# A planner's row of background work: a mark ends a slot only behind work, and four marks for a chunk instead of eight

## The chip, the core and the metric

The kernel runs on one core of a Trainium2 chip. What counts is the device time of one execution in microseconds (us). The core has a matrix engine (TensorE, in the rows PE for the matmuls and PEld for the loading of their stationary operand), a vector engine (VectorE, DVE), a scalar engine (ScalarE, ACT), a general one (GpSimd, POOL) and a queue that starts the DMAs (SyncE, SP). Each engine works off its own queue in program order, and semaphores make it wait for the others.

## The reference, cut to what matters

Three stages follow one another: an attention with 32 memory slots for each head, a feed-forward stage, and a stage of four experts, in which every token goes through every expert. Only the last is touched here:

```python
def _moe2_ref(x, domain_probs, w1, w2):      # x 2304 x 512, w1 4 x 512 x 1024, w2 4 x 1024 x 512
    p = domain_probs / (domain_probs.sum(-1, keepdims=True) + 1e-09)
    out = np.zeros((N, D), dtype=np.float32)
    for e in range(E):
        h = np.maximum(x @ w1[e], 0.0)
        out += p[:, e:e + 1] * (h @ w2[e])
    return out
```

## The kernel before, in words

All matmuls work on numbers that are split in two: a high part `hi` that TensorE takes in its fast format, which ScalarE writes with a cast, and the rest `lo`, which VectorE writes by subtracting `hi` from the number. A product of two split numbers is three matmuls (`PASSES`): hi by hi, hi by lo, lo by hi. So every weight needs a `hi` on ScalarE and then a `lo` on VectorE before its matmuls can run.

The expert stage goes through the tokens in three passes of 768 tokens (two halves of 384). A pass has eight chunks, so there are 24 chunks, n = 0 to 23: half of one expert's 1024 hidden columns each. A chunk consists of:

- two **units**, m = 2n and 2n+1 (`unit`). Each multiplies a 2 x 2 block of `w1` with the 2 x 2 block of x in the manner of Strassen, seven products instead of eight, each of six matmuls of 384 columns. The products come in the order b, a, c, d, a, c, d, named by the PSUM bank that they go to (`pb`, `pa`, `pc`, `pd`); the second ones of a, c and d add to what stands in their bank. Between them ScalarE copies bank b to `p` (L915), VectorE forms `u` twice (a plus p, then c plus that; L906) and the sums `cy`, `cx`, and the two engines make the eight `h` tiles of the chunk (L879, L880). The second product of a may start only when VectorE has read a for the first `u`.
- the **second** half (`second`): h by `w2`, six blocks of twelve matmuls of 512 columns, in PSUM tiles `po` (L954). After each block VectorE adds the scaled result to `oacc` (L962).

The weights are prepared beside this as background work. For a unit m these are the four casts `hi0`, `hi3`, `hi2`, `hi1` (L320), the four subtractions `lo0`, `lo3`, `lo2`, `lo1` (L323), and on GpSimd the four additions `s1`, `s3`, `s2`, `s4` (L326 to L335), which form from the raw blocks the sums that Strassen's scheme wants. `hi2` and `lo2` need s1 and s3, `hi1` and `lo1` need all four, and s1 may overwrite its block only when lo0 and lo3 have read theirs. For `w2` there are four casts (L351) and four subtractions (L355) a chunk. In the rows the tiles are `W_0` to `W_3` (or `pair`, where the half-size W_3 lies in a shared tile) and `w_n_q`. Four DMAs a chunk bring the raw weights into a ring of four buffers.

All these pieces stand in one list, `todo`, in an order written out by hand. `fill(t)` takes pieces from its head in a **slot**, until t us of VectorE time are used up or a mark (`gap`) comes. There are slots only at certain places of a chunk: one after the first product of a unit, b, and one after its second product, a (t = 0.6; the other five products have t = 0, with which `fill` does nothing), and one after each of the six blocks of the second half (t = 1.9). That makes ten slots a chunk. What is not yet done when it is needed is done at once by `need(key)`, which takes everything ahead of it from the list as well. A piece that needs a free weight slot and finds none also ends `fill`. A piece done in a slot lands on its engine's queue behind everything that stands there already.

Behind the last chunk of a pass, the x tiles of the next pass (`x_ops`, 18 pieces, L683, L686, L689) are put ahead of the list.

Of the kernel before, what the change touches and what calls it, by code (L numbers as in the profile page):

```python
# [126 lines left out]
def body(ctx: ExitStack, tc: tile.TileContext, phiT, kv, qT, w_in, w_out, w1, w2, dp, out):  # L127
# [635 lines left out]
    def add(key, t, ok, fn):  # L763
        todo.append((key, t, ok, fn))

    def go():
        key, t, ok, fn = todo.pop(0)
        assert ok(), key
        fn()
        made.add(key)  # L770
        return t

    def fill(t):
        while todo and t > 0 and todo[0][2]():
            if todo[0][0] == "gap":
                todo.pop(0)
                break
            t -= go()

    def need(key):  # L780
        while key not in made:
# [14 lines left out]
    def gap():  # L796
        todo.append(("gap", 0, yes, None))
# [3 lines left out]
    def add_unit(m, *names):  # L801
        if m not in steps_of:
            steps_of[m] = unit_ops(m)
        for name, eng, cost, fn in steps_of[m]:
            if name in names:
                ok = has_half if name == "hi3" else has_slot if eng == "A" else yes
                add((name, m), cost / 1e3 if eng == "V" else 0, ok, fn)

    def add_w2(step, n, x):
        for q in (2 * x, 2 * x + 1):  # L810
            add((f"w2{step}", n, q), 0.6 if step == "lo" else 0, has_slot if step == "hi" else yes,
                partial(w2_lo if step == "lo" else w2_hi, n, q))

    def load(fn, *a):

        if a[0] <= (last_n if fn is w2_load else 2 * last_n + 1):
            add(("load", fn.__name__, *a), 0, yes, partial(fn, *a))
# [9 lines left out]
    add_w2("hi", 0, 0)  # L827
    gap()
    add_unit(1, *B2)
    gap()  # L830
    add_w2("lo", 0, 0)
    load(w2_load, 1, 0)
    load(unit_load, 3)
    add_w2("hi", 0, 1)
    add_unit(2, *A1)
    gap()
    add_w2("lo", 0, 1)
    load(w2_load, 1, 1)
    gap()
    for n in range(1, last_n + 1):  # L840
        m = 2 * n
        add_unit(m, *A2)
        add_w2("hi", n, 0)
        gap()
        add_w2("lo", n, 0)
        gap()
        add_unit(m, *B1)
        add_unit(m + 1, *A1)
        gap()
        add_unit(m, *B2)  # L850
        load(unit_load, m + 2)
        load(w2_load, n + 1, 0)
        gap()
        add_unit(m + 1, *A2)
        add_w2("hi", n, 1)
        gap()
        add_w2("lo", n, 1)
        gap()
        add_unit(m + 1, *B1)
        if n < last_n:  # L860
            add_unit(m + 2, *A1)
        gap()
        add_unit(m + 1, *B2)
        load(unit_load, m + 3)
        load(w2_load, n + 1, 1)
        gap()

    late_lo = []

# [13 lines left out]
    def unit(n, u):  # L883
# [25 lines left out]
        def step(t):  # L909
            flush(1)  # L910
            fill(t)
# [29 lines left out]
    def second(n, half):  # L941
        p, c = divmod(n, NCE)
        e = c // (FF2 // CF)
        t = 2 * p + half
        if c == 0:
            oacc[t] = acc_slot(t, [P, TW // P, DM], f"oacc{t}")
        for q in range(4):
            need(("w2lo", n, q))
        for j in range(TW // P):
            ps = ps_acc.tile([P, DM], F32, tag=f"acc{blk[0] % 4}", name="po")  # L950
            blk[0] += 1
            for i in (0, 2, 3, 1):
                for k, (x, y) in enumerate(PASSES):
                    nc.tensor.matmul(ps, hts[n, i, half][0][:, x, j * P:(j + 1) * P], w2s[n, i][0][:, y],  # L954
                                     start=(i == 0 and k == 0), stop=(i == 1 and k == 2))
            flush(0)
            o, tt = oacc[t][:, j], t * (TW // P) + j
            sc = pr[:, tt, e:e + 1]
            if c == 0:
                nc.vector.tensor_scalar_mul(o, ps, sc)  # L960
            else:
                nc.vector.scalar_tensor_tensor(out=o, in0=ps, scalar=sc, in1=o, op0=ALU.mult, op1=ALU.add)  # L962
            if c == NCE - 1:
                nc.sync.dma_start(out=out[tt * P:(tt + 1) * P, :], in_=o)
            fill(1.9)
        for i in range(4):
            h_free.append(hts.pop((n, i, half))[1])
        if half == 0:
            for i in range(4):
                free_slots.append(w2s.pop((n, i))[1])  # L970
# [46 lines left out]
```

## Time and profile before

| what | value |
|---|---|
| three runs | 1214.91 us median, 1214.39 to 1219.59 |
| profiled execution, its own time | 1214.46 us |
| its span in the trace | 1212.7 us, of which the expert stage fills 391.8 to the end |
| TensorE | busy 1135.1 us, 94% of the span |
| VectorE, ScalarE, GpSimd | busy 849.9, 466.1 and 173.5 us |

The profiled execution is 0.45 us under the median, and its span is 1.8 us shorter than its own time, since a little lies before and behind the trace. TensorE's busy time counts overlapped matmuls, so what can be read from a stretch is the distance from one start to the next.

### The profile page before, as it was taken

How to read it: one execution, taken by the hardware profiler on the slowest of the kernel's cores; microseconds unless marked ns; L12 is line 12 of the kernel's file. 1: busy time of each engine (PE TensorE's matmuls, PEld its weight loads, DVE VectorE, ACT ScalarE, POOL GpSimd, SP SyncE). 2: the span in 40 equal slices, each digit the busy share in tenths (PEclk: the TensorE clock that was granted, in tenths of full speed). 3: DMA queues.
4: the chain of work that ended last, by engine and by line, in shares of the span. 5: the costliest groups of instructions: out<-in, count | busy, mean ns of one | idle time of the engine just before them, and what ended most of it. 6: DMA issues, size and time to landing. Idle time of an engine off the chain costs nothing. (4 is left out here: it accounts for less than half of the span.)

```text
span 1212.7 us, 16585 instructions
## 1 busy us (share of the span) xinstructions
PE 1135.1 (94%) x6488; PEld 1031.6 (85%) x6488; DVE 849.9 (70%) x1510; ACT 466.1 (38%) x918; POOL 173.5 (14%) x200
## 2 busy tenths in 40 slices
PE   4999999999999999999998799999998799999998
PEld 3789999999999788888887788888887788888887
DVE  7998999955576666666667666666667566666764
ACT  3665554433453333333333333333333333333331
POOL 0000000000110122122221221222221112222220
PEclk9999999999999999999999899999999799999999
DMA  9822222100000211212222111222212122121101
GB/s 358 318 96 74 89 86 74 67 18 1 19 1 1 70 54 69 70 70 70 70 69 88 38 68 70 70 70 70 70 53 91 49 70 70 70 70 59 64 18 53
DMA packets 31167, 89.46 MB, mean 74 GB/s; under 512 B 2928, under 2 KB 2928, under 8 KB 30576
## 3 DMA queue, kind: packets, MB, share of 16 engines
q1 hardware_dynamic: 31088, 88.39, 20.8%
q8 instruction: 51, 0.84, 0.3%
q14 instruction: 28, 0.23, 0.1%
HBM read 83.66 MB, written 4.72 MB: 73 GB/s over the span
## 5 line engine op out<-in xcount | busy, mean ns | idle before, releaser
L954 PE MATMUL po<-w,h 128*128 128x512 f32 x1728 | 397.1, 390 | 1.2 <-ACT w L351 1.0
L954 PEld LDWEIGHTS po<-w,h 128*128 128x128 f32 x1728 | 324.0, 188 | 68.3 <-ACT w L351 1.5
L648 PE MATMUL pacc<-g,w 128*128 128x384 f32 x1152 | 213.9, 337 | 0.9 <-DVE g L372 0.9
L648 PEld LDWEIGHTS pacc<-g,w 128*128 128x128 f32 x1152 | 198.9, 188 | 8.0 <-issue 5.9
L962 DVE SCALAR_TENSOR_TENSOR oacc<-po,pr,oacc 128x512 f32<-128x512 f32 x126 | 94.4, 750 | 132.1 <-PE po L954 129.8
L326 POOL TENSOR_TENSOR u_raw<-u_raw 128x256 f32<-128x256 f32 x48 | 36.4, 759 | 993.7 <-DVE pair L323 735.8
L320 ACT CAST W<-u_raw 128x512 fp32r<-128x512 f32 (+1 forms) x160 | 89.8, 599 | 139.1 <-POOL u_raw L329 82.2
L622 PE MATMUL ph<-attnT,u 128*128 128x384 f32 (+1 forms) x768 | 121.3, 306 | 0.1
L898 PE MATMUL pa<-xop,W 128*128 128x384 f32 x576 | 119.8, 344 | 0.0
L898 PE MATMUL pb<-xop,W 128*128 128x384 f32 x288 | 69.3, 365 | 53.5 <-DVE W L323 28.9
L898 PE MATMUL pc<-xop,W 128*128 128x384 f32 x576 | 117.8, 339 | 0.0
L622 PEld LDWEIGHTS ph<-attnT,u 128*128 128x128 f32 x768 | 112.4, 190 | 5.9 <-DVE g L372 1.7
L323 DVE TENSOR_TENSOR W<-u_raw,W 128x512 fp32r<-128x512 f32 (+1 forms) x160 | 105.7, 676 | 4.6 <-ACT W L320 4.1
L898 PEld LDWEIGHTS pb<-xop,W 128*128 128x128 f32 x288 | 52.3, 198 | 65.1 <-DVE W L323 37.0
L898 PEld LDWEIGHTS pa<-xop,W 128*128 128x128 f32 x576 | 105.8, 195 | 0.0
L898 PEld LDWEIGHTS pc<-xop,W 128*128 128x128 f32 x576 | 104.2, 193 | 0.0
L915 ACT COPY p<-pb 128x384 f32<-128x384 f32 x48 | 23.1, 482 | 202.0 <-PE pb L898 202.0
L355 DVE TENSOR_TENSOR w<-w2raw,w 128x512 fp32r<-128x512 f32 x96 | 89.3, 969 | 0.6 <-ACT w L351 0.6
L879 ACT ACTIVATE h<-cx 128x384 fp32r<-128x384 f32 x96 | 50.4, 525 | 78.0 <-DVE cx L906 78.0
L372 DVE TENSOR_TENSOR g<-t,g 128x384 fp32r<-128x384 f32 x96 | 53.2, 556 | 38.2 <-ACT g L369 38.0
L369 ACT CAST g<-t 128x384 fp32r<-128x384 f32 x96 | 49.4, 514 | 78.5 <-PE pacc L648 69.7
L898 PE MATMUL pd<-xop,W 128*128 128x384 f32 x384 | 76.9, 334 | 0.0
(92 smaller groups left out, 1236.5 us busy)
## 6 DMA issues: line engine op xcount, KB each, us to landing
u_raw<-in_w SPq DMA_DIRECT2D x48, 512.0 KB, 3.2
w2raw<-in_w SPq DMA_DIRECT2D x48, 512.0 KB, 3.3
raw<-in_w_in SPq DMA_DIRECT2D x16, 512.0 KB, 4.0
kv<-in_kv SPq DMA_DIRECT2D x16, 512.0 KB, 8.0
raw<-in_w_out SPq DMA_DIRECT2D x16, 512.0 KB, 3.3
q<-in_qT SPq DMA_DIRECT2D x4, 1152.0 KB, 7.5
out_y<-oacc SPq DMA_DIRECT2D x18, 256.0 KB, 2.0
phi<-in_phiT SPq DMA_DIRECT2D x4, 576.0 KB, 9.6
```

Source lines behind the costliest of these rows:

```text
L320: nc.scalar.copy(w[:, 0], r()[:, slice(*parts[k])])
L323: v(out=W[k][0][:, 1], in0=r()[:, slice(*parts[k])], in1=W[k][0][:, 0].bitcast(F32), op=ALU.subtract)
L326: g(out=r()[:, 2], in0=r()[:, 3], in1=r()[:, 2], op=ALU.add)
L355: nc.vector.tensor_tensor(out=w[:, 1], in0=w2raw[n, q // 2][:, q % 2], in1=w[:, 0].bitcast(F32), op=ALU.subtract)
L369: nc.scalar.copy(hi, src)
L372: nc.vector.tensor_tensor(out=lo, in0=src, in1=hi.bitcast(F32), op=ALU.subtract)
L622: nc.tensor.matmul(ps[:, o:o + m], uts[c, b][:, x, hq, i * P:(i + 1) * P], attnT[b][:, y, hq, s0:s0 + m], start=(k == 0), stop=(k == 5))
L648: nc.tensor.matmul(pacc[j][:, 0:TW], w[:, x, j * P:(j + 1) * P], g[:, y], start=(i == 0 and k == 0), stop=(i == NI - 1 and k == 2))
L879: nc.scalar.activation(h[:, 0], src, AF.Relu)
L898: nc.tensor.matmul(bk[b], W[k][0][:, xx, o, kt * P:(kt + 1) * P], xop[x][:, y, kt], start=first and kt == 0 and i == 0, stop=kt == 1 and i ...
L954: nc.tensor.matmul(ps, hts[n, i, half][0][:, x, j * P:(j + 1) * P], w2s[n, i][0][:, y], start=(i == 0 and k == 0), stop=(i == 1 and k == 2))
L962: nc.vector.scalar_tensor_tensor(out=o, in0=ps, scalar=sc, in1=o, op0=ALU.mult, op1=ALU.add)
```

## The change

A mark now ends a slot only if that slot has already done something; at the head of a slot a mark is skipped. And the list has four marks for a chunk instead of eight, at other places. In the list for the first chunk a few pieces and two loads stand in another order.

```diff
     def fill(t):
+        some = False
         while todo and t > 0 and todo[0][2]():
             if todo[0][0] == "gap":
                 todo.pop(0)
-                break
-            t -= go()
+                if some:
+                    break
+            else:
+                t -= go()
+                some = True
...
     add_unit(1, *B2)
-    gap()
-    add_w2("lo", 0, 0)
-    load(w2_load, 1, 0)
-    load(unit_load, 3)
     add_w2("hi", 0, 1)
     add_unit(2, *A1)
     gap()
+    add_w2("lo", 0, 0)
     add_w2("lo", 0, 1)
+    load(w2_load, 1, 0)
+    load(unit_load, 3)
     load(w2_load, 1, 1)
     gap()
     for n in range(1, last_n + 1):
...
         add_w2("hi", n, 0)
         gap()
         add_w2("lo", n, 0)
-        gap()
         add_unit(m, *B1)
         add_unit(m + 1, *A1)
         gap()
         add_unit(m, *B2)
         load(unit_load, m + 2)
         load(w2_load, n + 1, 0)
-        gap()
         add_unit(m + 1, *A2)
         add_w2("hi", n, 1)
         gap()
         add_w2("lo", n, 1)
-        gap()
         add_unit(m + 1, *B1)
         if n < last_n:
             add_unit(m + 2, *A1)
...
         load(unit_load, m + 3)
         load(w2_load, n + 1, 1)
-        gap()
```

(A1 is hi0 and hi3; A2 is lo0, lo3 and the four additions; B1 is hi2 and hi1; B2 is lo2 and lo1.)

The first place is VectorE's queue from the last product of unit 4 to the first products of unit 5, both in chunk 2; the queue stands alike in every later chunk that is not the first of a pass. Before:

```order
L906 TENSOR_TENSOR cx_4917<-pd,u_4_4868 128x384
L880 SCALAR_TENSOR_TENSOR h_0_1_4908<-cx_4906,h_0_1_4908 128x384
L323 TENSOR_TENSOR W_1_4856<-u_raw_4657,W_1_4856 128x512
L906 TENSOR_TENSOR u_5_4943<-pa,p_5_4930 128x384
L323 TENSOR_TENSOR W_0_4858<-u_raw_4801,W_0_4858 128x512
L906 TENSOR_TENSOR u_5_4953<-pc,u_5_4943 128x384
```

The same place with the change, where the lines of the file are one less:

```order
L905 TENSOR_TENSOR cx_4933<-pd,u_4_4884 128x384
L879 SCALAR_TENSOR_TENSOR h_0_1_4924<-cx_4922,h_0_1_4924 128x384
L355 TENSOR_TENSOR w_3_1_4875<-w2raw_0_4775,w_3_1_4875 128x512
L905 TENSOR_TENSOR u_5_4955<-pa,p_5_4945 128x384
L905 TENSOR_TENSOR u_5_4971<-pc,u_5_4955 128x384
L905 TENSOR_TENSOR cy_4980<-pd,u_5_4971 128x384
```

`W_1_4856` is lo1 of unit 5, which unit 5's first product reads. It no longer stands between the units; in its place stands a subtraction for w2 of the next chunk.

The second place is VectorE's queue ahead of that, in the last three blocks of the second half of chunk 1, up to the start of unit 4. Before:

```order
L962 SCALAR_TENSOR_TENSOR oacc_4502<-po,pr,oacc_4502 128x512
L323 TENSOR_TENSOR W_0_4781<-u_raw_4657,W_0_4781 128x512
L323 TENSOR_TENSOR W_3_4783<-u_raw_4657,W_3_4783 128x256
L962 SCALAR_TENSOR_TENSOR oacc_4502<-po,pr,oacc_4502 128x512
L355 TENSOR_TENSOR w_2_2_4825<-w2raw_1_4659,w_2_2_4825 128x512
L355 TENSOR_TENSOR w_2_3_4827<-w2raw_1_4659,w_2_3_4827 128x512
L906 TENSOR_TENSOR u_4_4868<-pa,p_4_4852 128x384
L323 TENSOR_TENSOR W_2_4854<-u_raw_4657,W_2_4854 128x512
```

With the change:

```order
L355 TENSOR_TENSOR w_2_2_4797<-w2raw_1_4659,w_2_2_4797 128x512
L355 TENSOR_TENSOR w_2_3_4799<-w2raw_1_4659,w_2_3_4799 128x512
L961 SCALAR_TENSOR_TENSOR oacc_4509<-po,pr,oacc_4509 128x512
L323 TENSOR_TENSOR W_2_4817<-u_raw_4657,W_2_4817 128x512
L323 TENSOR_TENSOR W_1_4819<-u_raw_4657,W_1_4819 128x512
L323 TENSOR_TENSOR W_0_4821<-u_raw_4773,W_0_4821 128x512
L323 TENSOR_TENSOR pair<-u_raw_4773,pair 128x256
L961 SCALAR_TENSOR_TENSOR oacc_4509<-po,pr,oacc_4509 128x512
L905 TENSOR_TENSOR u_4_4884<-pa,p_4_4871 128x384
```

Here lo2 and lo1 of unit 5 (`W_2_4817`, `W_1_4819`) and behind them lo0 and lo3 of unit 6 (`W_0_4821`, `pair`) stand in one slot, a whole unit ahead of unit 5; before, lo0 and lo3 of unit 5 (`W_0_4781`, `W_3_4783`) stood there.

The third place is the change of pass, at chunk 8 (unit 16), on ScalarE and on VectorE. ScalarE up to the copy `p` of unit 16, before:

```order
L351 CAST w_8_0_6470<-w2raw_0_6176 128x512
L351 CAST w_8_1_6472<-w2raw_0_6176 128x512
L320 CAST W_2_6491<-u_raw_6174 128x512
L320 CAST W_1_6493<-u_raw_6174 128x512
L320 CAST W_0_6495<-u_raw_6305 128x512
L320 CAST W_3_6497<-u_raw_6305 128x256
L915 COPY p_16_6508<-pb 128x384
```

With the change:

```order
L351 CAST w_8_2_6496<-w2raw_1_6201 128x512
L351 CAST w_8_3_6498<-w2raw_1_6201 128x512
L320 CAST W_2_6517<-u_raw_6199 128x512
L320 CAST W_1_6519<-u_raw_6199 128x512
L320 CAST W_0_6521<-u_raw_6486 128x512
L320 CAST pair<-u_raw_6486 128x256
L914 COPY p_16_6531<-pb 128x384
```

The casts ahead of the copy are now those of unit 17 (hi2, hi1) and 18 (hi0, hi3), where they were those of 16 and 17. And VectorE there with the change, from the last x tile on:

```order
L686 TENSOR_TENSOR xop_4077<-acc_1331,xop_4077 128x768
L323 TENSOR_TENSOR W_2_6330<-u_raw_6132,W_2_6330 128x512
L961 SCALAR_TENSOR_TENSOR oacc_4509<-po,pr,oacc_4509 128x512
L323 TENSOR_TENSOR W_1_6332<-u_raw_6132,W_1_6332 128x512
L323 TENSOR_TENSOR W_0_6334<-u_raw_6199,W_0_6334 128x512
L323 TENSOR_TENSOR W_3_6336<-u_raw_6199,W_3_6336 128x256
L961 SCALAR_TENSOR_TENSOR oacc_4509<-po,pr,oacc_4509 128x512
L355 TENSOR_TENSOR w_8_2_6496<-w2raw_1_6201,w_8_2_6496 128x512
L355 TENSOR_TENSOR w_8_3_6498<-w2raw_1_6201,w_8_3_6498 128x512
L323 TENSOR_TENSOR W_2_6517<-u_raw_6199,W_2_6517 128x512
L905 TENSOR_TENSOR u_16_6541<-pa,p_16_6531 128x384
```

`W_1_6332` is lo1 of unit 16. Before, the six rows behind the last x tile were lo3 of unit 16, the two `oacc`, two subtractions for w2 and lo2 of unit 16, and only then lo1 of unit 16.

## Rows read from the trace of the kernel before

**Rows 1.** The page, busy time by engine

```profile
PE 1135.1 (94%) x6488; PEld 1031.6 (85%) x6488; DVE 849.9 (70%) x1510; ACT 466.1 (38%) x918; POOL 173.5 (14%) x200
```

**Rows 2.** Groups by line: busy us, mean ns | idle before, releaser

```profile
L323 DVE TENSOR_TENSOR W<-u_raw,W 128x512 fp32r<-128x512 f32 (+1 forms) x160 | 105.7, 676 | 4.6 <-ACT W L320 4.1
...
L962 DVE SCALAR_TENSOR_TENSOR oacc<-po,pr,oacc 128x512 f32<-128x512 f32 x126 | 94.4, 750 | 132.1 <-PE po L954 129.8
L320 ACT CAST W<-u_raw 128x512 fp32r<-128x512 f32 (+1 forms) x160 | 89.8, 599 | 139.1 <-POOL u_raw L329 82.2 <-POOL u_raw L335 56.9
L355 DVE TENSOR_TENSOR w<-w2raw,w 128x512 fp32r<-128x512 f32 x96 | 89.3, 969 | 0.6 <-ACT w L351 0.6
...
L898 PE MATMUL pb<-xop,W 128*128 128x384 f32 x288 | 69.3, 365 | 53.5 <-DVE W L323 28.9 <-ACT W L320 24.6
...
L915 ACT COPY p<-pb 128x384 f32<-128x384 f32 x48 | 23.1, 482 | 202.0 <-PE pb L898 202.0
```

**Rows 3.** Timeline of TensorE in chunk 6: start, us, what, [idle before]

```profile
592.04 1.23 PE L898 MATMUL pb<-xop,W 128*128 128x384 f32 x6
...
599.34 0.51 PE L898 MATMUL pb<-xop,W 128*128 128x384 f32 x2
...
601.22 0.96 PE L898 MATMUL pb<-xop,W 128*128 128x384 f32 x4 [1.36 <-DVE W L323]
...
605.16 1.20 PE L898 MATMUL pa<-xop,W 128*128 128x384 f32 x6
...
608.28 16.52 PE L954 MATMUL po<-w,h 128*128 128x512 f32 x72
...
624.64 0.69 PE L898 MATMUL pb<-xop,W 128*128 128x384 f32 x3
```

**Rows 4.** Timeline of TensorE: first and last of 20 like waits

```profile
470.83 0.97 PE L898 MATMUL pb<-xop,W 128*128 128x384 f32 x4 [1.37 <-DVE W L323]
...
1184.97 0.97 PE L898 MATMUL pb<-xop,W 128*128 128x384 f32 x4 [1.37 <-DVE W L323]
```

**Rows 5.** Timeline of VectorE beside the wait of rows 3

```profile
599.54 0.56 DVE L906 TENSOR_TENSOR cx<-pd,u 128x384 f32<-128x384 f32 x1
600.01 0.55 DVE L880 SCALAR_TENSOR_TENSOR h<-cx,h 128x384 fp32r<-128x384 f32 x1
...
600.48 0.68 DVE L323 TENSOR_TENSOR W<-u_raw,W 128x512 fp32r<-128x512 f32 x1
```

**Rows 6.** Timeline of TensorE in chunk 1

```profile
426.16 1.23 PE L898 MATMUL pb<-xop,W 128*128 128x384 f32 x6
...
445.29 16.52 PE L954 MATMUL po<-w,h 128*128 128x512 f32 x72
```

**Rows 7.** Timeline of TensorE at both changes of pass

```profile
640.89 16.52 PE L954 MATMUL po<-w,h 128*128 128x512 f32 x72
...
662.26 2.37 PE L898 MATMUL pb<-xop,W 128*128 128x384 f32 x6 [4.84 <-ACT W L320]
...
687.75 4.51 PE L954 MATMUL po<-w,h 128*128 128x512 f32 x19
...
915.96 16.52 PE L954 MATMUL po<-w,h 128*128 128x512 f32 x72
...
963.82 6.55 PE L954 MATMUL po<-w,h 128*128 128x512 f32 x28
```

**Rows 8.** Windows: busy by engine (x rows), granted clock, DMA share, GB/s

```profile
662.20:666.20 4.00, 3.91 (x12) 3.51 (x13) 0.69 (x1) 1.32 (x4) 0.00 (x0) 0.57 0.68 247
```

**Rows 9.** Timeline at the first change of pass: VectorE, GpSimd

```profile
656.35 0.96 DVE L686 TENSOR_TENSOR xop<-acc,xop 128x768 fp32r<-128x768 f32 x1 [0.95 <-ACT xop L683]
...
657.77 0.72 POOL L326 TENSOR_TENSOR u_raw<-u_raw 128x256 f32<-128x256 f32 x1 [29.83 <-DVE pair L323]
...
660.51 1.05 POOL L335 TENSOR_TENSOR u_raw<-u_raw 128x256 f32<-128x256 f32 x1
```

**Rows 10.** The page, DMA issues: KB each, us from issue to landing

```profile
u_raw<-in_w SPq DMA_DIRECT2D x48, 512.0 KB, 3.2
```

## The prediction, made before the changed kernel ran

> **What bounds the kernel now.** I began with the page. TensorE is busy for 94% of the span [rows 1], so a change of the background work can gain only what TensorE waits for, or runs slowly after a wait. The groups by line say where the expert stage waits: ahead of the first product of a unit, `pb`, 53.5 us in all, ended by VectorE's subtractions for W (28.9) and by ScalarE's casts for W (24.6) [rows 2]. TensorE's timeline then shows when. In a steady chunk the even unit runs without a wait, from 592.04 to 599.34: 7.30 us. The odd unit starts at 599.34, gets two matmuls in, and stands for 1.36 us; the unit takes until 608.28, 8.94 us. The second half takes 16.36 (608.28 to 624.64) [rows 3]. So a chunk is 32.60, and without the wait it would be 30.96. The wait costs 1.64, the pipeline's restart counted in. There are 20 such chunks, in all but n = 0, 1, 8 and 16 [rows 4].
>
> VectorE's timeline beside the wait shows its cause. Behind the last product VectorE forms `cx` at 599.54, then an h tile, then lo1 of the odd unit from 600.48, which ends at 601.16; TensorE goes on at 601.22 [rows 5, 3]. VectorE isn't overloaded there: lo1 merely stands behind work that itself waits for the unit's last product. That is `need`: lo1 hadn't come up in any slot.
>
> The other chunks lose more. Unit 2 and 3 of chunk 1 take 19.13 us (426.16 to 445.29) instead of 2 x 7.30 = 14.60: 4.5 lost [rows 6]. At the first change of pass the second half ends at 640.89 + 16.36 = 657.25, and the units 16 and 17 last until 687.75: 30.50, so 15.9 are lost. At the second it is 915.96 + 16.36 = 932.32 to 963.82: 31.50, and 16.9 lost [rows 7]. Part of that is the clock: behind the wait of 4.84 us the granted clock is 0.57 for 4 us, between the levels 1.2 and 2.4 GHz, and 12 matmuls take 4.0 us [rows 7, 8] where 12 of a steady unit take 2 x 7.30 / 7 = 2.1: 1.9 us. Behind the steady 1.36 there is nothing of the kind: five products on, the pace is as before (601.22 to 605.16) [rows 3].
>
> **The change, part by part.** The number of casts, subtractions, additions and DMAs stays; only slots change.
>
> *Steady chunks.* Now every odd unit's lo2 and lo1 stand in the second half of the chunk before, a whole unit early, and TensorE's wait has no cause left. What takes lo1's place is a subtraction for w2 of the next chunk. It is 0.97 us at the mean [rows 2], and what stands behind it is the odd unit's first `u`. Is that late? VectorE starts `cx` 0.20 behind the odd unit's start [rows 3, 5]; successive rows of VectorE start some 0.09 before the one ahead ends [rows 5], so cx, the h tile and w2's subtraction are through by 0.20 + 0.47 + 0.46 + 0.97 = 2.1. `u` needs the second product anyway, done at some 2.1 + 0.2. It ends at 2.9, and TensorE wants bank a again at 4 x 1.04 = 4.2: 1.3 us to spare.
>
> The slot with the longest work is now oacc with lo2, lo1, lo0 and lo3, under 0.75 + 4 x 0.68 = 3.5 against 16.36 / 6 = 2.73 for a block. VectorE ends 0.8 late in the next block, whose slot holds nothing for it, and four `po` tiles lie between it and TensorE: no wait. (0.75 for oacc and 0.68 for each subtraction [rows 2, 5]; lo3 is half the size.) GpSimd's four additions start behind that slot and last some 3.8 (657.77 to 660.51 + 1.05) [rows 9]: through 7.5 us into the half. The four casts behind them, 4 x 0.60 [rows 2], end at some 10, and the next copy `p` is due at 16.36 / 6 x 5 + 1.04 = 14.7: 4.7 to spare on ScalarE. The DMAs: the raw tile's load is issued one slot or more earlier than its cast's slot and lands in 3.2 us [rows 10]; at the closest, load in one block and cast two blocks on, 5.4 lie between. So 20 x 1.64 = **32.8 us** go.
>
> *Chunk 0* keeps its waits: lo1 of unit 1 is still done by `need`, and VectorE still makes three w2 subtractions just ahead of the first second half. I count nothing.
>
> *Chunk 1.* lo1 of unit 3 moves into a slot of unit 2, so the wait at unit 3 goes. But hi1 of unit 3 and two more casts stand in the last slot ahead of unit 2, and `p` of unit 2 behind them on ScalarE. VectorE's lo0 and lo3 of unit 3 end some 3.5 into block 4, GpSimd 3.8 later at 7.3, hi1, hi0, hi3 at 9.0, `p` (0.48 [rows 2]) at 9.5, `u` at 10.1; TensorE wants bank a at 2 x 2.73 + 4.2 = 9.7. Counted from the end of block 4, that makes 0 to 1.5 us, since the 3.5 is an upper bound; I take 0.3, and 4.5 - 0.3 = **4.2** go.
>
> *Changes of pass.* Here the wait doesn't vanish, it moves. VectorE ends the last x tile at 656.35 + 0.87 = 657.2 in the queue's steps [rows 9], as before. Now lo2 of unit 16 follows (0.59), oacc (0.66) and lo1: done at some 659.2, not behind two w2 subtractions and lo2. TensorE, free at 657.25, does two matmuls and waits until 659.2 instead of 662.26: some 1.7 lost with the restart. Next late is `p`. Behind lo1 stand lo0 and lo3 of unit 17 (to 660.1); GpSimd's additions for unit 17 wait for lo3 and end 3.8 later, at 663.9; hi1, hi0 and hi3 on ScalarE end at 665.6, `p` at 666.1, `u` at 666.6. hi0 also needs a load issued at some 658.6, landed at 661.8 [rows 10], so in time. TensorE would want bank a 3.94 behind its restart [rows 3], at 663.1, and gets it at 666.7: 3.6 lost. Unit 17 then finds lo1 ready. Whether the clock falls behind 3.6 us no row says: behind 4.84 it did, for 1.9 us, behind 1.36 not [rows 7, 8, 3]. 3.6 is nearer to 4.84, so I take 1.9. A change of pass so loses 1.7 + 3.6 + 1.9 = 7.2. Gains: 15.9 - 7.2 = 8.7 and 16.9 - 7.2 = 9.7, **18.4** together. Bounds for one change of pass: 1.7 (`p` in time) to 12 (the chain twice as late, or a second wait at unit 17).
>
> Two pages of the Trainium skill bear on this. GPSIMD Engine Reference, Specifications, says that GpSimd shares its SBUF interfaces with VectorE and contends with VectorE instructions that have two SBUF inputs. The rows agree: L335 takes 1.05 where L326 takes 0.72, and L355 0.97 where lo1 takes 0.68 [rows 9, 2, 5]. Two such subtractions stand beside the chain at the change of pass; were all four additions held to 1.05, the chain would be 4.4 and the sum 1.2 us smaller; were none, 3.1 and 1.4 larger. TensorE: Matmul & The Clock Gate, Part 1, says that half the clock is the default and activity has to release it, which speaks for paying the 1.9 again; without it the sum would be 3.8 larger. All of these lie within the forecast's own range below.
>
> *Sum.* 32.8 + 4.2 + 18.4 = 55.4. The profiled execution took 1214.46 (0.45 under the median): 1214.5 - 55.4 = **1159 us**.
>
> **The rivals.**
> - *The waits come back elsewhere.* The w2 subtraction, or a longer slot, makes a `u` late by more than the 1.3 to spare, and TensorE waits for bank a in every odd unit. For it: VectorE is at 70% and its slots are fuller. Against it: the two reckonings above. If the whole 1.64 came back: 1159 + 32.8 = 1192; half: 1175.
> - *Slower: `p` behind the GpSimd chain in every chunk.* What I expect at the two changes of pass would happen 20 times, if the additions of the odd unit ended 4.7 us later than reckoned. Price 3.6 + 1.9 = 5.5 a chunk, 110 us: 1269. From 55.4 / 20 = 2.8 us a chunk it is slower than before. Against it: in the rows ScalarE already waits for GpSimd (82.2 and 56.9 us [rows 2]) without TensorE noticing in a steady chunk.
> - *The changes of pass cost less.* `p` comes in time, or the clock holds: 1159 - 3.8 = 1155, at best 1159 - 11.0 = 1148.
> - *No change.* The new order only shifts which lo is last, and TensorE waits as long at another product. Against it: nothing in the list is then done by `need` in a steady chunk, so it would take a full VectorE. 1214.
>
> **How the numbers follow.** The forecast, with 1153 to 1166 as its own range: 0.74. Cheaper changes of pass: 0.08. Waits back in part or whole, 1166 to 1195: 0.11. No change: 0.03. Slower: 0.04. The range of 1149 to 1176 takes in the bounds of a change of pass (1.7 to 12, so -11 to +10), chunk 1's 1.5 and half of the steady wait. Half a per cent, 6 us, is about what a measurement of this kernel can tell from no change. Faster by more: 0.93; within: 0.03; slower: 0.04.
>
> **What would show it.** Right: no wait at `pb` in a steady chunk, and 31.0 us from one second half to the next instead of 32.6; units 2 and 3 together under 15.5; at a change of pass a wait of some 1.5 at `pb` ended by VectorE, then one of 3 to 4 at `pa` that ends with `u`, with GpSimd's additions and hi1 ahead of `p`, a clock under 1 behind it, and no wait at unit 17; L355's mean under 0.97, since it lies less beside GpSimd. Wrong: waits at `pa` or `pc` in the steady chunks, ScalarE's `p` far behind `pb`, or `po` waiting for a w2 subtraction.

## The result, and the profile after

The changed kernel takes **1158.6 us** (median of 4 runs, 1157.7 to 1160.18) beside 1217.25 us for the kernel before (4 runs, 1214.39 to 1219.78): a ratio of 0.952, 95% interval 0.949 to 0.955. Its profiled execution took 1160.18 us, with a span of 1158.4. Line numbers behind the fill rule have moved by a few: L898 of before is L897, L906 is L905, L915 is L914, L954 is L953, L962 is L961.

The page of the changed kernel, busy time by engine, answers to [rows 1]:

```profile
PE 1123.4 (97%) x6488; PEld 1027.2 (89%) x6488; DVE 821.6 (71%) x1510; ACT 463.4 (40%) x918; POOL 150.3 (13%) x200
```

The groups by line (busy us, mean ns of one, idle time before and its releasers) answer to [rows 2]:

```profile
L897 PE MATMUL pa<-xop,W 128*128 128x384 f32 x576 | 116.5, 336 | 7.2 <-DVE u L905 7.2
...
L355 DVE TENSOR_TENSOR w<-w2raw,w 128x512 fp32r<-128x512 f32 x96 | 65.1, 703 | 0.0
L897 PE MATMUL pb<-xop,W 128*128 128x384 f32 x288 | 59.0, 338 | 4.3 <-DVE W L323 4.3
...
L335 POOL TENSOR_TENSOR u_raw<-u_raw 128x256 f32<-128x256 f32 x48 | 38.8, 808 | 3.8
```

The reader is to see three things. The idle time ahead of `pb` went from 53.5 to 4.3, and ScalarE's share of it (24.6) is gone. There are 7.2 us at `pa` that were not there before. And L355, which VectorE does as often as before, takes 0.70 instead of 0.97 us: in most places it no longer lies beside GpSimd's additions, of which the last two got shorter too (at the mean L332 0.78, before 1.01, and L335 0.81, before 1.05; L326 and L329 stay near 0.76).

TensorE's timeline of chunk 6 answers to [rows 3]:

```profile
583.15 1.23 PE L897 MATMUL pb<-xop,W 128*128 128x384 f32 x6
...
590.45 1.20 PE L897 MATMUL pb<-xop,W 128*128 128x384 f32 x6
591.49 1.20 PE L897 MATMUL pa<-xop,W 128*128 128x384 f32 x6
...
594.61 1.20 PE L897 MATMUL pa<-xop,W 128*128 128x384 f32 x6
...
597.73 4.51 PE L953 MATMUL po<-w,h 128*128 128x512 f32 x19
```

Both units take 7.30 and 7.28 us; no row of a steady chunk has a wait. The next chunk begins at 614.09, so a chunk is 30.94 to 30.95 us instead of 32.60.

VectorE in the odd unit of that chunk:

```profile
590.65 0.56 DVE L905 TENSOR_TENSOR cx<-pd,u 128x384 f32<-128x384 f32 x1
591.13 0.55 DVE L879 SCALAR_TENSOR_TENSOR h<-cx,h 128x384 fp32r<-128x384 f32 x1
591.59 0.68 DVE L355 TENSOR_TENSOR w<-w2raw,w 128x512 fp32r<-128x512 f32 x1
592.79 0.56 DVE L905 TENSOR_TENSOR u<-pa,p 128x384 f32<-128x384 f32 x1 [0.51 <-ACT W L320]
```

The w2 subtraction stands where lo1 stood [rows 5], and the `u` behind it waits for its own product (pa, from 591.49 for 1.20, so to 592.69; the cast that the row names as its releaser is no input of it) and ends at 593.35. TensorE wants bank a at 594.61: 1.26 us to spare.

TensorE's timeline at the first change of pass answers to [rows 7]:

```profile
645.04 0.51 PE L897 MATMUL pb<-xop,W 128*128 128x384 f32 x2
647.00 0.97 PE L897 MATMUL pb<-xop,W 128*128 128x384 f32 x4 [1.46 <-DVE W L323]
647.81 1.20 PE L897 MATMUL pa<-xop,W 128*128 128x384 f32 x6
648.85 1.20 PE L897 MATMUL pc<-xop,W 128*128 128x384 f32 x6
649.89 1.20 PE L897 MATMUL pd<-xop,W 128*128 128x384 f32 x6
654.67 2.29 PE L897 MATMUL pa<-xop,W 128*128 128x384 f32 x6 [3.58 <-DVE u L905]
656.76 1.83 PE L897 MATMUL pc<-xop,W 128*128 128x384 f32 x6
658.43 1.20 PE L897 MATMUL pd<-xop,pair 128*128 128x384 f32 x6
...
666.75 1.55 PE L953 MATMUL po<-w,h 128*128 128x512 f32 x6
```

Two waits, at `pb` for lo1 and at `pa` for `u`; then six matmuls that take 2.09 us (654.67 to 656.76) and six that take 1.67 where 1.04 is the pace; then nothing. The windows of that stretch and of the like one in the second change of pass show the granted clock between its two levels of 1.2 and 2.4 GHz (0.61 and 0.65, the third number from the end):

```profile
654.60:659.00 4.40, 4.33 (x16) 4.33 (x17) 2.58 (x6) 1.01 (x2) 0.00 (x0) 0.61 0.37 123
909.30:914.00 4.70, 4.64 (x18) 4.57 (x19) 3.21 (x7) 1.43 (x3) 0.00 (x0) 0.65 0.36 112
```

Why `u` is late, on GpSimd, ScalarE and VectorE:

```profile
648.02 0.74 POOL L326 TENSOR_TENSOR u_raw<-u_raw 128x256 f32<-128x256 f32 x1 [33.02 <-DVE W L323]
648.84 1.07 POOL L329 TENSOR_TENSOR u_raw<-u_raw 128x256 f32<-128x256 f32 x1
...
651.13 1.05 POOL L335 TENSOR_TENSOR u_raw<-u_raw 128x256 f32<-128x256 f32 x1
...
649.94 0.62 ACT L320 CAST W<-u_raw 128x512 fp32r<-128x512 f32 x1 [4.80 <-POOL u_raw L329]
652.21 1.14 ACT L320 CAST W<-u_raw 128x512 fp32r<-128x512 f32 x2 [1.65 <-POOL u_raw L335]
653.25 0.40 ACT L320 CAST pair<-u_raw 128x256 fp32r<-128x256 f32 x1
653.56 0.47 ACT L914 COPY p<-pb 128x384 f32<-128x384 f32 x1
...
654.06 0.56 DVE L905 TENSOR_TENSOR u<-pa,p 128x384 f32<-128x384 f32 x1 [2.46 <-ACT p L914]
```

The product for `p` was done near 648, but the copy stands behind four casts, two of which wait for GpSimd. VectorE has idle time (2.46) and waits for the copy.

**Where the time came from.** From the stage's first product to the end of the span it was 391.82 to 1212.7 = 820.9 us, and is 394.20 to 1158.4 = 764.2: 56.7 gained. The span shows 54.3, because the stages ahead of the expert stage, which the change doesn't touch, took 2.4 us longer in this execution. So below I count from the first product. (The medians lie 58.7 apart, since two of the four executions of the kernel before took 1219.6 and 1219.8, some 5 us more than the traced one.)

### The profile page after: what moved, and what is told of

Read it like the earlier page. It is cut to its first block, busy times and chain, and to the rows that moved or that the text cites. A ratio compares the mean times of both kernels' runs of the same rounds, so it can differ in the third digit from the quotient of the medians.

```text
span 1158.4 us, 16603 instructions
## 1 busy us (share of the span) xinstructions
PE 1123.4 (97%) x6488; PEld 1027.2 (89%) x6488; DVE 821.6 (71%) x1510; ACT 463.4 (40%) x918; POOL 150.3 (13%) x200
## 5 line engine op out<-in xcount | busy, mean ns | idle before, releaser
L953 PE MATMUL po<-w,h 128*128 128x512 f32 x1728 | 396.8, 390 | 1.4 <-DVE w L355 1.4
L953 PEld LDWEIGHTS po<-w,h 128*128 128x128 f32 x1728 | 323.9, 188 | 68.2 <-DVE w L355 1.8
L961 DVE SCALAR_TENSOR_TENSOR oacc<-po,pr,oacc 128x512 f32<-128x512 f32 x126 | 94.3, 748 | 113.6 <-PE po L953 113.6
L326 POOL TENSOR_TENSOR u_raw<-u_raw 128x256 f32<-128x256 f32 x48 | 36.2, 755 | 954.1 <-DVE pair L323 690.8
L897 PE MATMUL pa<-xop,W 128*128 128x384 f32 x576 | 116.5, 336 | 7.2 <-DVE u L905 7.2
L897 PE MATMUL pc<-xop,W 128*128 128x384 f32 x576 | 116.7, 337 | 0.0
L897 PEld LDWEIGHTS pa<-xop,W 128*128 128x128 f32 x576 | 102.1, 189 | 7.8 <-DVE u L905 7.8
L897 PEld LDWEIGHTS pc<-xop,W 128*128 128x128 f32 x576 | 102.5, 190 | 0.1
L323 DVE TENSOR_TENSOR W<-u_raw,W 128x512 fp32r<-128x512 f32 (+1 forms) x160 | 97.5, 661 | 1.2 <-ACT W L320 0.9
L914 ACT COPY p<-pb 128x384 f32<-128x384 f32 x48 | 23.1, 481 | 141.8 <-PE pb L897 141.5
L897 PE MATMUL pd<-xop,W 128*128 128x384 f32 x384 | 77.7, 337 | 0.0
L628 ACT ACTIVATE t<-ph,three 128x384 f32<-128x384 f32 x96 | 55.9, 582 | 52.9 <-DVE g L372 44.0
L897 PEld LDWEIGHTS pd<-xop,W 128*128 128x128 f32 x384 | 68.4, 190 | 0.0
L355 DVE TENSOR_TENSOR w<-w2raw,w 128x512 fp32r<-128x512 f32 x96 | 65.1, 703 | 0.0
```

The lines of the kernel that those rows point to most:

```text
L323: v(out=W[k][0][:, 1], in0=r()[:, slice(*parts[k])], in1=W[k][0][:, 0].bitcast(F32), op=ALU.subtract)
L355: nc.vector.tensor_tensor(out=w[:, 1], in0=w2raw[n, q // 2][:, q % 2], in1=w[:, 0].bitcast(F32), op=ALU.subtract)
L628: nc.scalar.activation(t, st["ph", n], AF.Relu, bias=three, scale=1.0)
L897: nc.tensor.matmul(bk[b], W[k][0][:, xx, o, kt * P:(kt + 1) * P], xop[x][:, y, kt], start=first and kt == 0 and i == 0, stop=kt == 1 and i ...
```

## The experiments

They are numbered, and "run 3" is the kernel of the third. Each ratio is to the kernel before on the same chip (1215.33 us at the median beside the first four, 1215.46 beside the last four).

**1. The new fill rule alone**, with the eight marks of before:

```
+        some = False
...
-                break
-            t -= go()
+                if some:
+                    break
+            else:
+                t -= go()
+                some = True
```

> The kernel before with the new rule alone (a mark ends a slot only behind work), its eight marks and their places kept. Theory (the place of lo1 in VectorE's queue decides): the rule lets exactly one piece, a w2 subtraction of chunk 0, come up earlier; every lo1 of an odd unit still waits for need, so the 20 waits of 1.36 at pb and both changes of pass stay: ratio to before 1.000, within 0.003. Rival (the empty slots were what cost): the ten slots are now all used, and a good part of the 57 us goes: ratio 0.96 to 0.98.

Measured: 1218.08 us, ratio 1.001 (0.9992 to 1.0028), and the same waits as before: 53.6 us at `pb`, L355 at 968 ns. From the stage's first product to the end it is 821.1 us (396.71 to 1217.8), before 820.9. The rule does nothing by itself, and the new list with the old rule gives, instruction for instruction, the same program as the whole change (so that kernel wasn't run). So the change is the list: four marks at other places, and the few pieces of the first chunk in another order.

**2. Only lo1 of the odd unit early, in the kernel before.** The even unit's second slot is made longer in the 20 steady chunks, so that lo1 of the odd unit is done in it:

```
-        step(0.6)
+        step(0.6 if u or n < 2 or n % NCE == 0 else 1.2)
```

> The kernel before, rule and marks kept; only the second slot of the even unit takes 1.2 us instead of 0.6 in the 20 steady chunks, so that lo1 of the odd unit is done there, right behind lo2, six products ahead of its use. Theory (place of lo1): 20 x 1.7 = 34 us go, ratio 0.972; the changes of pass and chunk 1 lose as before (15.9, 16.9 and 4.5 us); L355's mean stays near 0.97 us. Rival (what gained was less contention of VectorE with GpSimd, L355's mean 0.97 before and 0.70 with the change): L355 stays at 0.97, so nearly nothing goes, ratio 0.995 or more.

Measured: 1185.9 us, ratio 0.9753 (0.9721 to 0.9784). The steady waits are gone and those at the changes of pass stay, as the groups by line show for `pb`; L355 keeps its length:

```profile
L355 DVE TENSOR_TENSOR w<-w2raw,w 128x512 fp32r<-128x512 f32 x96 | 89.2, 968 | 0.6 <-ACT w L351 0.6
L898 PE MATMUL pb<-xop,W 128*128 128x384 f32 x288 | 63.5, 357 | 26.2 <-ACT W L320 24.6 <-DVE W L323 1.6
```

A steady chunk is 31.04 us there (590.70 to 621.74): 20 x 1.56 = 31.2, and from the stage's first product to the end it is 31.8 less than before (396.72 to 1185.8 = 789.1). That is some 2 to 3 us under the 34 expected, which took 1.7 a chunk. So the place of one subtraction gives nearly all of the steady gain, without the rest of the new order. That L355 gets shorter gives TensorE next to nothing: here it stays at 968 ns, and a chunk is 0.09 longer than in the change.

**3. The reverse: lo1 put back, in the changed kernel.** In the 20 steady chunks lo1 of the odd unit is taken out of the list and done behind the even unit's last product, where it stood before (one load of w2 goes with it, since it reuses the buffer):

```
+            if name == "lo1" and m % 2 and m > 3 and m % (2 * NCE) != 1:
+                held[m] = fn
...
+        if m in held:
+            held.pop(m)()
+            if n < last_n:
+                w2_load(n + 1, 1)
+        else:
+            need(("lo1", m))
```

> The changed kernel, with lo1 of the odd unit in 20 steady chunks put back behind the even unit's last product (and one load for w2 behind it, since it takes that buffer). Theory (place of lo1): the wait of about 1.4 at pb is back 20 times, 34 us above the changed kernel's 1158.6: 1190 to 1196, ratio to before 0.977 to 0.983, with L355's mean still near 0.70. Rival (less contention): L355 stays at 0.70, so the time stays within 5 us of 1159, ratio 0.951 to 0.956.

Measured: 1193.22 us, ratio 0.9819 (0.9789 to 0.9849). TensorE's timeline in chunk 6:

```profile
594.17 0.51 PE L900 MATMUL pb<-xop,W 128*128 128x384 f32 x2
596.05 0.97 PE L900 MATMUL pb<-xop,W 128*128 128x384 f32 x4 [1.37 <-DVE W L323]
```

The wait is back, a chunk is 32.60 again, while L355 stays at 705 ns. With run 2 that settles it: the steady 33 us hang on where lo1 stands; the rest of the new order adds 0.09 a chunk.

**4. The x tiles' work of the next pass later**, behind s4 of the next odd unit instead of at the head of the list, so that GpSimd's additions for it don't wait behind the x tiles:

```
+            pos = [k for k, *_ in todo].index(("s4", 2 * n + 3)) + 1
             for name, eng, cost, fn in reversed(x_ops(p + 1)):
-                todo.insert(0, ((name, p + 1), cost / 1e3 if eng == "V" else 0, yes, fn))
+                todo.insert(pos, ((name, p + 1), cost / 1e3 if eng == "V" else 0, yes, fn))
```

> The changed kernel, with the 18 x pieces of a new pass put behind s4 of the next odd unit instead of at the head of the list: lo2, lo1 of unit 16 and lo0, lo3 and the four additions of unit 17 come a half earlier. Theory (at a change of pass TensorE waits for lo1 behind the x tiles, then for u, since p stands behind hi1 and hi1 behind GpSimd's additions): the wait of 1.46 at pb goes, p follows its product at once, the 3.58 at pa shrinks to 0 to 1.5 us, since VectorE has some 17.5 us of work in a half of 16.4, and the clock stays up: 7.5 us lost per change of pass become 0 to 2, 11 to 15 us less than the changed kernel, 1144 to 1148. Rival (VectorE is simply full in the last half of a pass, and the order only moves the wait): the u is as late as before, 3 to 4 us, and the time within 4 us of 1159.

Measured: 1158.05 us, ratio 0.9516 (0.9485 to 0.9548). The wait at `pb` went, but `pa` still waits for 2.75 us, and the clock still falls behind it (0.62 in the 4 us that follow). From the start of the last second half to the next one it is 35.37 and 35.55 us at the two changes, 38.07 and 38.09 in the change: 5.2 gained in all, where 11 to 15 were expected. The time itself is what the rival told, within 4 us of 1159: the traced execution entered the stage 3.1 us later than the change's (397.31, there 394.20). GpSimd and VectorE in that run show why the gain is small:

```profile
638.65 1.34 POOL L329 TENSOR_TENSOR u_raw<-u_raw 128x256 f32<-128x256 f32 x1
...
638.27 2.53 DVE L686 TENSOR_TENSOR xop<-acc,xop 128x768 fp32r<-128x768 f32 x2
640.73 1.49 DVE L689 TENSOR_TENSOR acc<-acc,acc 128x768 f32<-128x768 f32 x1
...
654.09 0.68 DVE L323 TENSOR_TENSOR W<-u_raw,W 128x512 fp32r<-128x512 f32 x1
654.70 0.55 DVE L905 TENSOR_TENSOR u<-pa,p 128x384 f32<-128x384 f32 x1
```

The additions now lie beside the x tiles' operations and both get longer: an addition 1.34, where the first of the chain in the change took 0.74 (at 648.02) and the next 1.07, L686 about 1.26 each where three take 2.69 away from GpSimd, L689 1.49 instead of 0.95. No cast waits for the additions here (the last one ends at 642.82); what the stretching costs is VectorE's time, 3.87 us for two L686 and one L689 (638.27 to 642.14) where the change takes 2.60 (632.31 to 634.91), and with it the last x tile comes later. And the order on ScalarE was wrong as well: the four casts still stood ahead of `p`, now behind the last x tile's cast, which waits for VectorE (L689 at 649.45), and two w2 casts, so `p` came at 654.13. VectorE was no earlier: it had no idle time ahead of this `u`, which follows its L323 of 654.09 at once. So a `p` in time would not have been enough, and in this order the rival's full VectorE is a part of the cause.

**5. The change again**, beside the next three.

> The changed kernel once more, beside the next three. Both theories: 1158 us, a ratio of 0.952 to the kernel before; from chunk 0's first wait to the end of the span 755; at both changes of pass a wait of 1.46 at pb and one of 3.58 at pa.

Measured: 1162.11 us, ratio 0.9539 (0.9512 to 0.9566), 755.1 us from chunk 0's first wait to the end, waits of 1.46 and 3.57 or 3.58 at both changes of pass.

**6. The copy `p` ahead of the casts.** One more mark, ahead of hi2 of unit 17 and its like in the next pass:

```
+            todo.insert([k for k, *_ in todo].index(("hi2", 2 * n + 3)), ("gap", 0, yes, None))
```

> The change, with one more mark at the two changes of pass, ahead of hi2 of unit 17, so that hi2, hi1, hi0 and hi3 come behind the copy p of unit 16 on ScalarE. Theory (the wait of 3.58 us at pa is p standing behind casts that wait for GpSimd's additions): p follows its product at once, the wait at pa falls from 3.58 to under 0.5, and lo1 of unit 17 becomes late instead: a wait of 1.5 to 2.5 at that unit's pb. A change of pass then loses some 4 us and not 7.5: 755 becomes 748, the time 1152. Rival (u is late because VectorE is full there, p or no p): the wait at pa stays at 3 to 4 us, and the new wait at unit 17 comes on top: 755 or more, 1158 to 1163.

Measured: 1156.73 us, ratio 0.9501 (0.9477 to 0.9525), 753.1 from chunk 0's first wait. ScalarE, VectorE and TensorE at the first change of pass:

```profile
646.96 0.48 ACT L914 COPY p<-pb 128x384 f32<-128x384 f32 x1 [3.20 <-PE pb L897]
...
649.01 0.55 DVE L905 TENSOR_TENSOR u<-pa,p 128x384 f32<-128x384 f32 x1
...
649.61 1.31 PE L897 MATMUL pa<-xop,W 128*128 128x384 f32 x6
...
655.85 0.97 PE L897 MATMUL pb<-xop,W 128*128 128x384 f32 x4 [2.38 <-DVE W L323]
656.66 1.94 PE L897 MATMUL pa<-xop,W 128*128 128x384 f32 x6
658.40 2.07 PE L897 MATMUL pc<-xop,W 128*128 128x384 f32 x6
```

The theory's places came out as told: `p` follows its product, `pa` waits for nothing, and lo1 of unit 17 is late by 2.38. That rules out, for the change's order, the rival of a VectorE that is full there. The price was not as told: 1.0 us gained at a change of pass (37.17 and 37.04 against 38.06 and 38.15 in the run beside it), not 3.5. (The medians lie 5.4 apart, the two traced executions 2.0, counted from chunk 0's first wait too; where the rest lies, in executions without a trace, isn't shown.) I had counted no loss of clock behind a wait of 2.4; there is one, six matmuls take 1.74 and 1.91 instead of 1.04, 1.6 us together.

**7. The order at the changes of pass written for what waits there.** The x tiles' work stands behind s4 of unit 17, the casts of units 17 and 18 ahead of its last three pieces, and lo2, lo1 and the w2 work in slots of the chunk behind:

```
+            pos = [k for k, *_ in todo].index(("s4", m)) + 1
...
+            todo[pos:end + 1] = [*xs[:-3], *casts, *xs[-3:], mark, *lows, *for_w2]
...
-            fill(1.9)
+            if not (c == NCE - 1 and p + 1 < NP and half == 0 and j == 2):
+                fill(1.9)
...
-        step(0.6)
+        step(0 if m in (2 * NCE, 4 * NCE) else 0.6)
...
-        step(0)
+        step(0.6 if m in (2 * NCE, 4 * NCE) else 0)
```

> The change, with the order at the two changes of pass written for what waits there: the x tiles' work right behind s4 of unit 17, the casts of units 17 and 18 ahead of its last three pieces, lo2 and lo1 of unit 17 and the w2 work in slots of the chunk behind. Theory: the wait at pb (1.46) goes, since the last x tile is done within the second half, and the wait at pa shrinks from 3.58 to 1 to 1.5, which is too short for the clock to fall; a change of pass loses 1.5 to 2 us and not 7.5. 755 becomes 743 to 744, the time 1147. Rival (as in the run with the x tiles' work moved alone, GpSimd's additions and the x tiles' subtractions stretch each other and the casts stay late): the wait at pa stays at 2.5 to 3, 750, the time 1154.

Measured: 1151.43 us, ratio 0.9454 (0.9427 to 0.948), 743.7 from chunk 0's first wait, 11.4 less than the change beside it. TensorE at both changes, and the windows behind the waits:

```profile
650.24 1.34 PE L897 MATMUL pa<-xop,W 128*128 128x384 f32 x6 [1.22 <-DVE u L905]
...
899.16 1.32 PE L897 MATMUL pa<-xop,W 128*128 128x384 f32 x6 [0.94 <-DVE u L905]
```

```profile
650.20:654.20 4.00, 3.96 (x22) 3.78 (x23) 3.41 (x7) 1.13 (x3) 0.00 (x0) 1.00 0.48 166
899.10:903.10 4.00, 3.94 (x22) 3.73 (x23) 3.41 (x8) 1.11 (x3) 0.00 (x0) 1.00 0.48 167
```

No wait at `pb`, a short one at `pa`, the clock at 1.00. A change of pass costs 1.6 and 1.3 us now (32.58 and 32.30 less 16.36 and 14.60), 7.1 in the change. The row met the expectation (743 to 744); the median lies 4.4 above the 1147 told, the traced execution, at 1148.5, 1.5.

**8. The same, and chunk 0's even unit with a longer second slot**, so that lo1 of unit 1 is done in it:

```
-        step(0.6)
+        step(0.6 if n else 1.2)
```

> As the run with the order at the changes of pass rewritten, and the even unit's second slot of chunk 0 is 1.2 us, so that lo1 of unit 1 is done there and the w2 subtractions ahead of the first second half come earlier. Theory: the wait of 1.37 at unit 1's pb goes, and perhaps the wait of 1.39 at po behind it: 1.6 to 3 us less than that run, 741 to 742 from the same row, the time 1144 to 1145. Rival (the work that was late there is late at the next product instead): the same time as that run, with the waits of chunk 0 at other tiles.

Measured: 1148.85 us, ratio 0.9437 (0.9409 to 0.9464). The wait of 1.37 at `pb` is gone and the one at `po` went from 1.40 to 0.79:

```profile
409.24 7.10 PE L953 MATMUL po<-w,h 128*128 128x512 f32 x30 [0.79 <-DVE w L355]
```

From the stage's first product to this row it is 392.80 to 409.24 = 16.44 us; with the chunk as it was, 393.81 to 412.51 = 18.70 in the run ahead. 2.3 us, as expected. This kernel has the lowest median of all, but its interval overlaps that of run 7, so the 2.3 us rest on these rows and not on the ratios. The median lies 4 us above the time told, the traced execution, at 1145.26, next to it.

## Why the prediction was right

- **Steady chunks, 20 x 1.64 = 32.8.** They gave 20 x (32.60 - 30.95) = 33.0. Runs 2 and 3 show the cause from both sides. The step on the work that takes lo1's place held too: `u` was to end 2.9 us behind the odd unit's start with 1.3 to spare, and it ended 2.90 behind (593.35 - 590.45) with 1.26 to spare. The w2 subtraction took 0.68 and not 0.97, which changed nothing, because `u` waited for its product in any case.
- **Chunk 0, nothing; chunk 1, 4.2.** Chunk 0 gave 0.1. Units 2 and 3 take 428.41 to 443.00 = 14.59 us, so the whole 4.5 went; the 0.3 that I left for a late `u` wasn't needed. The 0 to 1.5 around it had no working: by the prediction's own figures, 10.1 less 9.7, it is 0.4 at most.
- **Changes of pass, 7.2 lost in each, 18.4 gained.** The stretch of second half and two units went from 46.86 to 38.07 and from 47.86 to 38.09: 8.8 and 9.8, or 18.6, and 7.1 are still lost. By terms, in the rows of the first change: 1.7 at `pb` (1.46 and the restart: 645.04 to 647.81 less 1.04), predicted 1.7; 3.7 at `pa` (649.89 to 654.67 less 1.04), predicted 3.6, although GpSimd's additions took 4.16 (648.02 to 652.18) and not 3.8, since three of the four took 1.05 to 1.07 beside L355; clock 1.7 (2.09 and 1.67 less 2 x 1.04), predicted 1.9. The choice that the clock falls behind 3.6 us was right; the prediction says that no row tells it, but one did (below). The Trainium skill, TensorE: Matmul & The Clock Gate, Part 1, holds that half the clock is the default and has to be lifted by activity. The windows at 0.61 and 0.65 agree, in that the clock is down behind the wait and up again by the next unit; the waits of 1.46, behind which nothing slows, show that not every wait brings it down.
- **The sum, 55.4.** The stage gave 33.0 + 0.1 + 4.5 + 18.6 = 56.2, and 0.4 more behind the last second half's start (1192.02 to 1212.7 = 20.7, now 1138.09 to 1158.4 = 20.3): 56.6, by the ends of the stage 56.7 as counted above. That 1159 met 1158.6 so closely owes something to chance, since the stages ahead took 2.4 us more in the profiled execution.
- **The rivals.** No row at `pa`, `pc` or `po` of a steady chunk has a wait, so neither did the waits come back nor did `p` fall behind GpSimd's chain outside the changes of pass. There it did, as run 6 shows by taking the casts away from ahead of it. In the steady half the reckoning "through 7.5 us into the half" is 3.5 + 3.8 = 7.3 and counts from the end of the half's first block. The additions end 6.4 behind it (606.90, the block at 600.46), and ScalarE then stands idle for 7.0 us ahead of `p`, more than the 4.7 to spare.

Two places in the trace of the kernel before bear on the changes of pass and on the clock, and the prediction doesn't use them:

```profile
435.87 0.62 PE L898 MATMUL pb<-xop,W 128*128 128x384 f32 x2 [2.23 <-ACT W L320]
...
437.57 2.12 PE L898 MATMUL pa<-xop,W 128*128 128x384 f32 x6
439.49 1.80 PE L898 MATMUL pc<-xop,W 128*128 128x384 f32 x6
...
677.96 2.38 PE L898 MATMUL pb<-xop,W 128*128 128x384 f32 x6 [6.34 <-ACT W L320]
```

In chunk 1, behind a wait of 2.23 and one of 0.19, six matmuls took 1.92 us and six more 1.64 (437.57, 439.49, 441.13), 1.5 over the pace, at a granted clock of 0.55. So a row did show the clock falling behind less than 3.6 us, and 1.5 of chunk 1's 4.5 were clock. And at the first change of pass unit 17 stood for 6.34 us and lost 2.5 more to slow matmuls behind: 9.0 of the 15.9 lost there, the restart counted in. That unit gave the whole gain. It now starts without a wait, as predicted ("finds lo1 ready"); unit 16 lost 6.9 us before and loses 7.1 now, so there the wait only moved. At the second change it is 9.4 us of the 9.8 gained.

My own reckonings for further gains were less sure than the prediction. Run 4 missed its own because both `p` and VectorE's queue came to `u` only behind the last x tile, made later by the stretching, and run 6 because the clock falls behind 2.4 us too, as chunk 1 of the kernel before had shown.

## What to carry to other kernels

When TensorE waits a fixed bit in every chunk, look on the engine that releases it at what stands ahead of the late instruction: here VectorE was 70% busy, and one subtraction behind work that itself waited for TensorE cost 33 us. In a queue filled from a list, the marks decide that, so read the order as it comes out rather than the rule. Where a wait moves to another engine, follow the chain to its next link (here additions, casts, a copy, a subtraction) and price that before moving the first.

## What the runs showed of the hardware that I had not expected

- What a fall of the clock costs was nearly the same behind waits of 2.2 to 3.6 us: 1.5 behind 2.23, 1.6 behind 2.38, 1.5 behind 2.75 (655.30 to 658.86 in run 4, less 2 x 1.04), 1.7 behind 3.58. Behind longer waits, in the kernel before, it was more, and not the same for like waits: 1.9 behind 4.84 [rows 7, 8] and 2.5 behind 4.85 (937.33 to 942.98, less 3 x 1.04), 2.5 behind 6.34 and 2.9 behind 6.35. Behind 0.94, 1.22, 1.36 and 1.46 there was none, and no wait of the expert stage lies between 1.46 and 2.23. So in these runs shortening a wait from 3.6 to 2.4 gives back only the wait, and from 2.4 to 1.2 the clock as well.
- Behind the second change's wait the clock fell later: the first six matmuls took 1.16 us, the next two sixes 1.80 and 1.86 (909.36, 910.52, 912.32, 914.18). The loss was the same.
- GpSimd's additions and VectorE's subtractions of two SBUF tiles stretch each other. An addition takes 0.74 where VectorE does mostly an `oacc` (648.02), 1.07 beside L355 (648.84; in the kernel before up to 1.28, at 625.51) and 1.34 beside L686 or L689 (run 4).
- The stages ahead of the expert stage vary between executions, in code that is the same: the stage began at 391.21 in run 3 and at 397.31 in run 4. The granted clock near the start goes with it. From 18 to 43 us it was 0.93 in the kernel before and in run 3 (the stage began at 391.8 and 391.2), 0.86 in the change and in runs 5, 6 and 8 (392.8 to 394.2), 0.80 in run 7 (393.8) and 0.66 in runs 1, 2 and 4 (396.7 to 397.3). Behind its first product the change took 764.2 us and, in run 5, 764.3. Of the 4 to 7 us between the executions of one kernel most can be that; those without a trace don't show it.
